# Attention, routed experts and a softplus feed-forward in one kernel: weight-chunk loads, splits and one elementwise operation moved at the joint of the last two stages

## Chip, cores and metric

The kernel runs on one core of one Trainium2 chip. The metric is the device time of one execution in microseconds. Three runs of the kernel before gave 645.68, 647.77 and 648.97 us; their median is 647.77 us.

## What is computed

```python
attn_out = _attn_ref(q, k, v)                    # 2 batches, 8 heads, 576 positions, 64 wide, rotary
x = attn_out.transpose(0, 2, 1, 3).reshape(1152, 512)
x = _moe_ref(x, w_gate, w_noise, noise, w1, w2)  # 8 experts, best 2 of each token: relu(x @ w1[e]) @ w2[e]
# _moe2_ref(x, w_in, w_out): w_in 512 x 2048, w_out 2048 x 512
h = x @ w_in
g = np.maximum(h, 0.0) + np.log1p(np.exp(-np.abs(h)))
return (g @ w_out).astype(np.float32)
```

All products are made to float32 accuracy by splitting both operands into a high part (rounded to fp32r) and a low part (the rest), and adding three products: high by high, high by low, low by high.

## The kernel before, in words

The work is emitted in program order, and each engine runs its own instructions strictly in that order. TensorE (PE) multiplies, ScalarE (ACT) makes high parts and copies out of PSUM, VectorE (DVE) makes low parts, GpSimd (POOL) issues the gathers, and SyncE (SP) issues the loads.

**Weight chunks.** Weights arrive as 80 chunks of 512 KB, numbered 0 to 79: 64 of the experts, and from 64 on 16 of the feed-forward part, which come from the DRAM table `wtab`. `load_chunk` (L149) issues the load of the next chunk into one of 4 buffers `wraw`. `split_hi` (L179) makes the high part on ACT (L189) and queues the low part; `split_lo` (L198) makes the queued low part on DVE (L193) and then calls `load_chunk`, because a `wraw` buffer is free again. Chunk s goes to one of 11 places `w`/`wb`; chunks 75 to 79 go to a pool `wc`. `hold_loads` (L169) makes `load_chunk` only count calls; `let_loads` (L173) issues a small read of `yg` on SP, which waits for the gather of that tile, and then makes up the counted loads.

**The last expert run.** Nine runs of an expert each do eight steps `gemm1(r, f)` and then `gemm2(r, t, part)`, three parts for each tile of 128 rows. After each step `slot()` (L1496) makes the queued low part, and splits the next chunk if it is loaded and below a limit; in the last run the limit lets chunks up to 70 be split. In the last run's step f = 3 three gathers are issued; at f = 5 the loads are held. At the end of tile 0 two more gathers are issued (they read rows that the tile has just put to the DRAM table `ytab`), at the end of tile 1 the loads are let go, in tile 2 the first two token tiles are combined (L1535) and turned (`x2_T`, L1538) into the high and low parts `xh`, `xl` of the feed-forward part's first input.

**The feed-forward part.** Nine token tiles are taken as four groups c of 2, 3, 2 and 2 tiles (`CH`). Before its loop POOL gets three gathers of the next tiles (L1657 to L1660), two of which wait for the last rows put to `ytab`. The loop index n walks through (c, f), f = 0 to 15. In iteration n the program emits: `act2` of n-1 on DVE (L1623, which frees the PSUM buffer, and L1624); now and then a combine or a turn of a coming token tile, which also emits two gathers on POOL; `ff1_` of n (12 matmuls on PE, into one of 3 PSUM buffers `ph`, then Abs, Exp and Ln on ACT); `act3` of n-1 (the high part `gh` on ACT, L1630); `act1` of n (L1618 and L1619: with a = exp(-|h|) it makes u = (a + 1) - 1 and then a - u, which corrects the rounding of Ln's argument); the low part `gl` of n-1 on DVE (L1632); the queued low part of a chunk (L193); one `split_hi` while chunks are left; and `ff2_` of n-3 (six matmuls where the group has two tiles). So chunks 71 to 79 are split in iterations 0 to 8.

Of the kernel before, what the change touches and what calls it, by code (L numbers as in the profile page):

```python
# [18 lines left out]
OP = mybir.AluOpType  # L19
# [13 lines left out]
NR = len(CAPS)  # L33
# [72 lines left out]
def fused_kernel(ctx: ExitStack, tc: tile.TileContext, q, k, v, w_gate, w_noise, noise, w1, w2,  # L106
                 w_in, w_out, cs_t, out):
    nc = tc.nc
# [20 lines left out]
    chunk_src = []  # L129
# [17 lines left out]
    nxt = {"load": 0, "split": 0, "order": False, "held": None}  # L147
# [21 lines left out]
    def hold_loads():  # L169

        nxt["held"] = 0
# [26 lines left out]
    def split_lo():  # L198
        while lo_q:
            lo_q.pop(0)()  # L200
# [918 lines left out]
    for g in range(2 * NP_):  # L1119
        p, h = divmod(g, 2)  # L1120
        for u in range(6 - h):
            n = 5 * g + (0, 1, 2, 3, 3, 4)[u]
# [7 lines left out]
        for a in range(2):  # L1130
            n = 5 * g + 3 + a
# [4 lines left out]
        n = 5 * g + 5  # L1136
# [13 lines left out]
    for p in range(NP_):  # L1150
        n = 10 * p
# [100 lines left out]
    def weights(r):  # L1252
        return max(r - 1, 0)

    def xg_T(r, t):
        if t == 0:
            XT[r] = (mx.tile([128, 4, CAP], F32R, name="xh"), mx.tile([128, 4, CAP], F32R, name="xl"))
        xh, xl = XT[r]
        g = XG.pop((r, t))
        m = min(CAPS[r] - 128 * t, 128)  # L1260
        ps = psA.tile([128, 4, 128], F32, name="pa")[:, :, :m]
        for d in range(4):
            nc.tensor.transpose(ps[:, d, :], g[:m, d * 128:(d + 1) * 128], ident[:m, :m])  # L1263
        dh, dl = xh[:, :, t * 128:t * 128 + m], xl[:, :, t * 128:t * 128 + m]
        nc.scalar.activation(dh, ps, AF.Copy)
        nc.vector.tensor_tensor(out=dl, in0=ps, in1=dh.bitcast(F32), op=OP.subtract)  # L1266

    def gemm1(r, f, pool):
        xh, xl = XT[r]
        cap = CAPS[r]  # L1270
        ps = ps1.tile([128, CAP], F32, name="p1")[:, :cap]
        mm3(ps, [(w1_blk(weights(r), kk, f), (xh[:, kk, :cap], xl[:, kk, :cap])) for kk in range(4)], True, True)
        hb = pool.tile([128, 2 * CAP], F32R, name="hb", bufs=8)

        m = cap % 128 if 0 < cap % 128 <= 64 else 0
        n = cap - m
        hh, hl = hb[:, 0:cap], hb[:, cap + m:cap + m + n]
        HT[f] = hh, hl, hb[:, n:n + 2 * m]
        nc.scalar.activation(hh, ps, AF.Relu)  # L1279
        for o, c in [(hl, slice(0, n))] + [(hb[:, cap:cap + m], slice(n, cap))] * (m > 0):  # L1280
            nc.vector.scalar_tensor_tensor(out=o, in0=ps[:, c], scalar=0.0, in1=hh[:, c].bitcast(F32), op0=OP.max,  # L1281
                                           op1=OP.subtract)

    def gemm2(r, t, part, pool):
        if part == 0:
            P2[0] = ps2.tile([128, DM], F32, name="p2")
        m = min(CAPS[r] - 128 * t, 128)
        ps = P2[0]
        c = slice(t * 128, t * 128 + m)
        fs = ((0, 1, 2), (3, 4, 5), (6, 7))[part]  # L1290
        if m > 64:
            mm3(ps[:m], [((HT[f][0][:, c], HT[f][1][:, c]), w2_blk(weights(r), f)) for f in fs], part == 0, part == 2)
        else:

            for f in fs:
                wh, wl = w2_blk(weights(r), f)
                if f == 7:
                    nc.tensor.matmul(ps[:m], HT[f][0][:, c], wl, start=False, stop=False)
                nc.tensor.matmul(ps[:2 * m], HT[f][2], wh, start=f == 0, stop=f == 7)  # L1299
                if f < 7:  # L1300
                    nc.tensor.matmul(ps[:m], HT[f][0][:, c], wl, start=False, stop=False)  # L1301
        if part < 2:
            return
        y = ya[t] if r == 0 else pool.tile([128, DM], F32, name="y", bufs=2)
        if r + 1 == NR:
            Y8[t] = y
        if m > 64:
            nc.scalar.activation(y[:m], ps[:m], AF.Copy)
        else:
            nc.scalar.activation(y[:m], ps[m:2 * m], AF.Copy)  # L1310
            nc.vector.tensor_tensor(out=y[:m], in0=ps[:m], in1=y[:m], op=OP.add)
        r0 = (NOV + ROW0[r] + t) * 128

        def put():
            nc.scalar.dma_start(out=ytab[r0:r0 + m, :], in_=y[:m])
        if m > 64:
            put()
        else:
            puts.append((slot_no[0] + 2, put))
# [147 lines left out]
    def gather(r):  # L1467
        for t in range(RTILES[r]):
            m = min(CAPS[r] - 128 * t, 128)
            XG[r, t] = mo.tile([128, DM], F32, name="xg", bufs=4)  # L1470
            gather_rows(XG[r, t][:m], idxr[:m, r - 2, t:t + 1])
# [5 lines left out]
    def turn():  # L1477
        ps = psA.tile([128, 4, 128], F32, name="pa")
        nc.tensor.transpose(ps[:, 0, :], to1, ident)
        nc.scalar.activation(toT, ps[:, 0, :], AF.Copy)  # L1480
# [15 lines left out]
    def slot(limit):  # L1496
        n = slot_no[0]
        slot_no[0] += 1
        split_lo()
        if n >= 8:  # L1500
            next(late, None)
        while puts and puts[0][0] <= n:
            puts.pop(0)[1]()
        todo = sorted(dec_at.get(n, []), key=lambda x: x[0] is dec_load)
        for fn, u in todo:
            if u < NDEC:
                fn(u)
        if all(fn is not dec_b for fn, _ in todo) and nxt["split"] < min(limit, nxt["load"]):
            split_hi()
# [4 lines left out]
    def ygather(i, kk):  # L1514
        nonlocal ygt
        if ygt is None:
            ygt = yg_tile().bitcast(F32)
        o = (i % 3 if kk == 0 else 3 + i % 2) * DM
        g = ygt[:, o:o + DM]
        near = (i, kk) == (1, 1)  # L1520
        top = (NOV + ROW0[NR - 1] + (1 if near else min(i + 1, CB) if kk else 0)) * 128
        nc.gpsimd.indirect_dma_start(out=g, out_offset=None, in_=ytab[0:top, :],  # L1522
                                     in_offset=bass.IndirectOffsetOnAxis(ap=near1 if near else yrow[:, i, kk:kk + 1], axis=0))
        YG[i, kk] = g
# [4 lines left out]
    def scale0(i):  # L1529
        a = YG[i, 0]  # L1530
        nc.scalar.activation(a, a, AF.Copy, scale=wts[:, i, 0:1])
# [28 lines left out]
    for r in range(1, NR):  # L1560
        e = weights(r)
        for f in range(8):
            gemm1(r, f, mo)
            if r == 3 and f == 0:
                for _ in late:
                    pass
                turn()
            if r + 1 == NR and f == 3:
                for i in range(CH[0] + 1):
                    ygather(i, 0)  # L1570
            if r + 1 == NR and f == 5:
                hold_loads()
            slot(min(8 * e + NSLOT + f // 2, 64 + NSLOT))
        for t in range(RTILES[r]):
            for part in range(3):
                gemm2(r, t, part, mo)
                if r + 1 < NR and (t, part) in when[:RTILES[r + 1]]:
                    xg_T(r + 1, when.index((t, part)))
                if r + 1 == NR:
                    for do in ends.get((t, part), []):  # L1580
                        do()
                slot(min(8 * e + NSLOT + 4, 64 + NSLOT))
        if r + 2 < NR:
            gather(r + 2)
# [30 lines left out]
    def act1(c, f):  # L1615

        ps, a, l, u = HS[c, f]
        nc.vector.tensor_scalar(u, a, 1.0, 1.0, op0=OP.add, op1=OP.subtract)  # L1618
        nc.vector.tensor_tensor(out=a, in0=a, in1=u, op=OP.subtract)  # L1619

    def act2(c, f):
        ps, a, l, u = HS[c, f]
        nc.vector.scalar_tensor_tensor(out=l, in0=ps, scalar=0.0, in1=l, op0=OP.max, op1=OP.add)  # L1623
        nc.vector.tensor_tensor(out=l, in0=l, in1=a, op=OP.add)  # L1624
# [44 lines left out]
    for n in range(len(seq) + FL):  # L1669
        if 1 <= n <= len(seq):  # L1670
            act2(*seq[n - 1])
        for i, u in extra.pop(n, []):
            if u == 0:
                scale0(i)
                combine(i)
            else:
                x2_T(i, psh.tile([128, 4, 128], F32, name="px", bufs=1))
                if i + 2 < NT:
                    ygather(i + 2, 0)
                    ygather(i + 2, 1)  # L1680
        if n < len(seq):
            ff1_(*seq[n])
        sub = act3(*seq[n - 1]) if 1 <= n <= len(seq) else None
        if n < len(seq):
            act1(*seq[n])
        if sub:
            sub()
        split_lo()
        if nxt["split"] < len(chunk_src):
            split_hi()  # L1690
        if n >= FL:
            c, f = seq[n - FL]
            for o in range(CH[c]):
                ff2_(c, f, o)
# [38 lines left out]
```

## Time and profile before

| | us |
|---|---|
| median of three runs | 647.77 |
| the profiled execution, its own time | 647.54 |
| its span, first to last instruction | 645.5 |
| PE busy | 624.0 (97%) |
| DVE busy | 482.2 (75%) |
| ACT busy | 424.3 (66%) |
| POOL busy | 211.7 (33%) |
| mean granted TensorE clock, share of full | 0.987 |

The profiled execution's time is 2.0 us more than its span and 0.2 us below the median. Busy matmul time is modelled, so a busy PE can still be waiting a little in each iteration. The chain of waits follows back from the last instruction to what released each step; a window table gives each engine's busy time and the granted clock in a stretch; a timeline lists instructions with their start and duration, and in brackets the idle time before them and what ended it.

### The profile page before, as it was taken

The page shows a single profiled execution, that of the slowest core. Times are in us where ns is not written, and L with a number is a line of the kernel's source. Part 1 is how long each engine was busy: PE and PEld are TensorE (multiplying, and loading weights), DVE is VectorE, ACT ScalarE, POOL GpSimd, SP SyncE. Part 2 cuts the span into 40 slices and gives each one's busy share as a digit, 9 for nine tenths or more (in the row PEclk, how much of TensorE's full clock was granted, in tenths as well). Part 3 has the DMA queues.
Part 4 walks back from the last instruction along what each step waited for, and adds up shares of the span by engine and source line. Part 5 has one row for each costly group of instructions (what it writes and reads, how often), then busy time and mean ns, then how long its engine had stood idle before and what let it go on. Part 6 is the DMA issues. An engine that isn't in the chain of part 4 may idle for free.

```text
span 645.5 us, 11587 instructions
## 1 busy us (share of the span) xinstructions
PE 624.0 (97%) x3957; PEld 560.0 (87%) x3957; DVE 482.2 (75%) x986; ACT 424.3 (66%) x893; POOL 211.7 (33%) x304
## 2 busy tenths in 40 slices
PE   6898999999999999999999999979999999999997
PEld 3798999999879889797988889868789989889986
DVE  5997899999876887686867776439986656676764
ACT  4986999899636677475757665438765554565553
POOL 7997636874271324323241414202110100000000
PEclk7998999999999999999999999989999999999999
DMA  5565655887419799989998997477211100100000
GB/s 132 139 143 133 160 119 129 234 242 214 136 53 356 232 354 336 319 276 344 315 336 292 330 307 231 140 256 210 87 34 50 33 1 1 49 2 2 34 2 32
DMA packets 69921, 109.59 MB, mean 170 GB/s; under 512 B 11716, under 2 KB 38980, under 8 KB 69476
## 3 DMA queue, kind: packets, MB, share of 16 engines
q1 hardware_dynamic: 63442, 93.20, 46.8%
q0 software_dynamic: 3136, 10.10, 4.7%
q10 hardware_dynamic: 3282, 5.54, 2.4%
q8 instruction: 32, 0.52, 0.3%
q14 instruction: 29, 0.24, 0.1%
HBM read 76.50 MB, written 23.59 MB: 155 GB/s over the span
## 4 chain that ended last, share of the span: by engine, by line
PE 63%; DVE 3%; DMA 2%; ACT 1%; issue 1%; POOL 0%; SPq 0%; DVEq 0%
PE p L270 10%; PE p L271 10%; PE p L272 10%; PE po L272 5%; PE ph L270 5%; PE po L271 5%; PE po L270 5%; PE ph L271 5%; PE ph L272 5%; PE p L1299 2%; PE pa L1263 1%; PE p L1301 1%; DMA wraw<-wtab 1%; DMA yg<-ytab,near 1%; DVE wb L193 1%
## 5 line engine op out<-in xcount | busy, mean ns | idle before, releaser
L239 POOL TENSOR_TENSOR dm<-dm,da 128x512 int32<-128x512 int32 x32 | 41.9, 1310 | 127.9 <-DVE da L236 63.3
L1611 ACT ACTIVATE fa<-ph 128x256 f32<-128x256 f32 (+1 forms) x64 | 26.0, 406 | 69.2 <-PE ph L272 69.2
L504 DVE TENSOR_REDUCE nmx<-ps 128x1 f32<-128x576 f32 x72 | 53.8, 750 | 8.5 <-PE ps L491 7.8
L193 DVE TENSOR_TENSOR w<-wraw,w 128x1024 fp32r<-128x1024 f32 x41 | 54.2, 1328 | 5.8 <-ACT w L189 5.8
L513 ACT ACTIVATE P<-ps,nmx 128x576 f32<-128x576 f32 x72 | 53.7, 745 | 3.0 <-DVE nmx L504 2.3
L1281 DVE SCALAR_TENSOR_TENSOR hb<-p,hb 128x256 fp32r<-128x256 f32 (+1 forms) x104 | 31.7, 345 | 30.3 <-ACT hb L1279 30.2
L1618 DVE TENSOR_SCALAR fu<-fa 128x256 f32<-128x256 f32 (+1 forms) x64 | 19.9, 311 | 45.9 <-ACT fa L1612 45.7
L189 ACT ACTIVATE w<-wraw 128x1024 fp32r<-128x1024 f32 x42 | 44.3, 1058 | 13.1 <-DMA wraw<-wtab 6.8
L558 DVE TENSOR_TENSOR ptl<-pt,pth 128x512 fp32r<-128x512 f32 x72 | 48.4, 684 | 5.0 <-ACT pth L554 4.5
L1522 POOL DMA_INDIRECT yg<-ytab,yrow x17 | 17.2, 1010 | 91.7 <-DVE fu L1618 42.5
L554 ACT ACTIVATE pth<-pt 128x512 fp32r<-128x512 f32 x72 | 42.4, 600 | 6.9 <-PE pt L522 6.4
L271 PE MATMUL p<-xl,w 128*128 128x256 f32 (+3 forms) x152 | 46.3, 305 | 0.3 <-DVE xl L1266 0.3
L270 PE MATMUL p<-xh,w 128*128 128x256 f32 (+3 forms) x152 | 46.3, 305 | 0.0
L272 PE MATMUL p<-xh,w 128*128 128x256 f32 (+3 forms) x152 | 46.2, 304 | 0.0
L193 DVE TENSOR_TENSOR wb<-wraw,wb 128x1024 fp32r<-128x1024 f32 x33 | 45.0, 1370 | 0.0
L522 PE MATMUL pt<-ident,P 128*128 128x128 f32 x288 | 42.7, 275 | 0.9 <-DVE ptl L558 0.6
L189 ACT ACTIVATE wb<-wraw 128x1024 fp32r<-128x1024 f32 x33 | 34.8, 1058 | 2.9 <-DMA wraw<-in_moe_w_dram 2.8
L1619 DVE TENSOR_TENSOR fa<-fa,fu 128x256 f32<-128x256 f32 (+1 forms) x64 | 29.4, 459 | 9.8 <-ACT fl L1613 7.1
L522 PEld LDWEIGHTS pt<-ident,P 128*128 128x128 f32 x288 | 34.3, 142 | 1.9 <-DVE ptl L558 1.1
L491 PE MATMUL ps<-wb,yg 128*128 128x288 f32 (+1 forms) x160 | 31.3, 325 | 3.1 <-DMA w<-in_v_dram 2.2
L1630 ACT ACTIVATE gh<-fl 128x256 fp32r<-128x256 f32 (+1 forms) x64 | 27.7, 432 | 9.4 <-DVE fl L1624 9.4
L1279 ACT ACTIVATE hb<-p 128x320 fp32r<-128x320 f32 (+3 forms) x64 | 25.7, 419 | 12.0 <-PE p L272 11.3
(387 smaller groups left out, 2170.0 us busy)
## 6 DMA issues: line engine op xcount, KB each, us to landing
wraw<-in_moe_w_dram SPq DMA_DIRECT2D x64, 512.0 KB, 4.9
x<-in_moe_w_in_dram SPq DMA_DIRECT2D x16, 512.0 KB, 6.4
x<-in_moe_w_out_dram SPq DMA_DIRECT2D x16, 512.0 KB, 4.7
wtab<-dm SPq DMA_DIRECT2D x32, 256.0 KB, 5.7
wraw<-wtab SPq DMA_DIRECT2D x16, 512.0 KB, 5.3
ytab<-y ACTq DMA_DIRECT2D x18, 256.0 KB, 5.4
ytab<-wb SPq DMA_DIRECT2D x4, 1024.0 KB
wb<-wb SPq DMA_DIRECT2D x6, 640.0 KB
```

What stands on the lines that cost most here:

```text
L189: nc.scalar.activation(hi, r, AF.Copy)
L193: lo_eng.tensor_tensor(out=lo, in0=r, in1=hi.bitcast(F32), op=OP.subtract)
L239: nc.gpsimd.tensor_tensor(out=m, in0=m, in1=ai, op=OP.add)
L270: nc.tensor.matmul(ps, ah, bh, start=first and i == 0, stop=False)
L271: nc.tensor.matmul(ps, ah, bl, start=False, stop=False)
L272: nc.tensor.matmul(ps, al, bh, start=False, stop=last and i == n - 1)
L504: nc.vector.tensor_reduce(out=nmx, in_=stS[n][:, :, :HN], axis=AX.XY, op=OP.max, negate=True)
L513: nc.scalar.activation(P_of(n).rearrange("p (a c) -> p a c", a=2), ps[:, :, :HN], AF.Exp, bias=nmx, scale=1.0, accum_out=acc)
L522: nc.tensor.transpose(ps[:, kb, :], Pt[:, kb * 128:(kb + 1) * 128], ident)
L554: nc.scalar.activation(dh, x, AF.Copy)
L558: nc.vector.tensor_tensor(out=dl, in0=x, in1=dh.bitcast(F32), op=OP.subtract)
L1281: nc.vector.scalar_tensor_tensor(out=o, in0=ps[:, c], scalar=0.0, in1=hh[:, c].bitcast(F32), op0=OP.max, op1=OP.subtract)
```

## The change

Three edits: the loads are held at step f = 7 of the last run instead of f = 5; for the first group (c = 0) the first operation of `act1` goes to GpSimd instead of VectorE; and in the feed-forward loop no chunk is split in iterations 1, 4, 7, ... The number of chunks and all arithmetic stay the same.

```diff
-            if r + 1 == NR and f == 5:
+            if r + 1 == NR and f == 7:
                 hold_loads()
...
     def act1(c, f):
         ps, a, l, u = HS[c, f]
-        nc.vector.tensor_scalar(u, a, 1.0, 1.0, op0=OP.add, op1=OP.subtract)
+        (nc.gpsimd if c == 0 else nc.vector).tensor_scalar(u, a, 1.0, 1.0, op0=OP.add, op1=OP.subtract)
         nc.vector.tensor_tensor(out=a, in0=a, in1=u, op=OP.subtract)
...
         split_lo()
-        if nxt["split"] < len(chunk_src):
+        if n % 3 != 1 and nxt["split"] < len(chunk_src):
             split_hi()
```

## Rows read from the trace of the kernel before

**Rows 1.** Windows: stretch, length, busy PE PEld DVE ACT POOL, clock, DMA share, GB/s.

```profile
431.70:440.44 8.74, 8.63 (x55) 8.02 (x55) 5.12 (x11) 5.54 (x12) 3.81 (x4) 0.83 0.67 198
440.44:478.40 37.96, 37.58 (x229) 31.07 (x230) 36.02 (x81) 29.74 (x67) 5.77 (x6) 1.00 0.38 116
478.40:630.00 151.60, 151.60 (x888) 137.28 (x887) 99.94 (x241) 82.29 (x193) 2.84 (x3) 1.00 0.06 18
```

**Rows 2.** Chain of waits before the feed-forward part: start us, us, what.

```profile
423.25 5.50 DMA wraw<-wtab
...
429.74 0.59 ACT xh L1551
...
431.69 0.58 PE ph L270
```

**Rows 3.** DMA issues of the page: chunk loads from the table, median us to landing.

```profile
wraw<-wtab SPq DMA_DIRECT2D x16, 512.0 KB, 5.3
```

**Rows 4.** PE timeline: start us, us, line, out<-in; three single matmuls.

```profile
427.70 0.40 PE L272 MATMUL p<-wb,hb 128*128 128x512 f32 x1
...
475.57 0.28 PE L270 MATMUL ph<-xh,wc 128*128 128x256 f32 x1
...
478.39 0.34 PE L270 MATMUL ph<-xh,wb 128*128 128x384 f32 x1
```

**Rows 5.** ACT timeline: the last expert tile's copy out of PSUM.

```profile
430.69 0.60 ACT L1308 ACTIVATE y<-p 128x512 f32<-128x512 f32 x1
```

**Rows 6.** POOL timeline: the third of the three gathers before the loop.

```profile
436.76 0.95 POOL L1522 DMA_INDIRECT yg<-ytab,yrow  x1 [0.30 <-DVE fl L1623]
```

**Rows 7.** POOL timeline: scalar operations, one operator (L1006, L661) and two (L1008, L707).

```profile
44.02 1.52 POOL L1006 TENSOR_SCALAR wb<-ident 128x512 fp32r<-128x512 f32 x1
45.60 0.20 POOL L1008 TENSOR_SCALAR kb<-iota 128x8 f32<-128x8 f32 x1
...
111.73 0.36 POOL L707 TENSOR_SCALAR c<-e 128x32 f32<-128x32 f32 x1
...
128.02 0.25 POOL L661 TENSOR_SCALAR kb<-isA 128x8 f32<-128x8 f32 x1
```

**Rows 8.** POOL timeline: two stretches in which DVE works beside it.

```profile
181.63 1.64 POOL L804 TENSOR_SCALAR P<-iotaA,P 128x128 f16<-128x128 f16 x1
183.25 0.60 POOL L804 TENSOR_SCALAR P<-iotaA,P 128x128 f16<-128x128 f16 x1
...
258.21 1.30 POOL L239 TENSOR_TENSOR dm<-dm,da 128x512 int32<-128x512 int32 x1 [2.84 <-ACT wb L189]
```

**Rows 9.** DVE timeline: low parts of chunks beside these.

```profile
181.66 1.22 DVE L193 TENSOR_TENSOR w<-wraw,w 128x1024 fp32r<-128x1024 f32 x1
...
258.86 1.74 DVE L193 TENSOR_TENSOR w<-wraw,w 128x1024 fp32r<-128x1024 f32 x1
```

**Rows 10.** DVE timeline: one iteration of the feed-forward loop in group c = 0.

```profile
450.07 0.42 DVE L1624 TENSOR_TENSOR fl<-fl,fa 128x256 f32<-128x256 f32 x1
450.42 0.28 DVE L1618 TENSOR_SCALAR fu<-fa 128x256 f32<-128x256 f32 x1
450.81 0.43 DVE L1619 TENSOR_TENSOR fa<-fa,fu 128x256 f32<-128x256 f32 x1
...
451.49 1.22 DVE L193 TENSOR_TENSOR wc<-wraw,wc 128x1024 fp32r<-128x1024 f32 x1
452.62 0.42 DVE L1623 SCALAR_TENSOR_TENSOR fl<-ph,fl 128x256 f32<-128x256 f32 x1
```

**Rows 11.** ACT timeline: one iteration of the feed-forward loop in group c = 0.

```profile
457.13 0.42 ACT L1630 ACTIVATE gh<-fl 128x256 fp32r<-128x256 f32 x1 [0.45 <-DVE fl L1624]
457.45 1.05 ACT L189 ACTIVATE wc<-wraw 128x1024 fp32r<-128x1024 f32 x1
458.41 0.36 ACT L1611 ACTIVATE fa<-ph 128x256 f32<-128x256 f32 x1
458.80 0.42 ACT L1612 ACTIVATE fa<-fa 128x256 f32<-128x256 f32 x1
```

## The prediction, made before the changed kernel ran

> **What bounds the kernel now.** I read the window table first. From 478.4 to 630 us PE is busy without a gap at full clock, and so it is nearly throughout: PE sets the end, and whatever delays it near the joint of the stages moves the end by as much [rows 1]. Two stretches beside the change are not of that kind. In 440.44 to 478.40, the first group (c = 0) from its fifth iteration to the first matmul of the second group, DVE is busy 36.0 of 38.0 us; here PE waits a little for DVE in most iterations [rows 1]. And the chain of waits leaves PE before the feed-forward part: it runs through a chunk load (5.50 us), a split on ACT, the copy to xh at 429.74, and reaches PE at 431.69 [rows 2], while PE's last product of the expert run began at 427.70 [rows 4]. ACT stands in its queue at the splits of chunks 69 and 70, whose loads were let go late, and the copies to xh are queued behind them. The gap also costs clock: from 431.70 to 440.44 the granted clock is 0.83 of full, that is, part of the stretch ran at 1.2 instead of 2.4 GHz, a loss of 0.17 x 8.74 = 1.5 us [rows 1].
>
> **Edit 1, loads held two steps later.** By index: at f = 5 of the last run the low part of chunk 65 is made, at f = 6 that of 66. Their calls now load chunks 69 and 70 at once. Slots then split 69 and 70 after the first two parts of tile 0, and the limit (70) stops there; 71 to 74 are the four loads let go. So the two splits leave ACT's queue ahead of xh. The loads take 5.3 us to land [rows 3], about the time of the tile's 24 products, so ACT may reach the split of 70 a little before it lands: 0 to 1 us on the copy of tile 0, and the two combines behind it had slack; I take 0. On SP the two loads pass the last store to the table, which only chunk 79 needs. With xh free, PE can go on right behind its last product, at about 427.9, since copies and differences of both tiles take 1.95 us in the chain [rows 2] and the first tile's are done beside PE. The start comes 3.7 us earlier, and no clock is lost there.
>
> **Edit 2, u on GpSimd.** First its place. POOL runs in order, and ahead of u(0) stand three gathers that wait for the last expert tile to reach DRAM. That tile's copy began at 430.69 and the first gather at 436.76 - 2 x 1.25 = 434.26, 3.6 us later, the third ending at 437.7 [rows 5, 6]. The copy can now start at about 428.1; so the gathers run from about 431.5 and POOL is free at 435.0. Before, none of that stood in DVE's way. Now a - u of iteration 0 waits on DVE, behind it act2(0), which frees the first of three PSUM buffers, and gh(0) on ACT: PE does three iterations (12 matmuls, 1.4 us each, to 432.2) and stops. With u at 1.25 us (below): u(0) ends at 436.2, DVE's next two operations 0.8 us later, and PE's fourth iteration starts at 437.2, after a gap of 5 us that is longer than the one which halved the clock before; I charge 1.3 us of half clock again. The fifth iteration would then start at 441.3 against 440.44: **the joint costs +0.9 us** in place of gaining about 5.
>
> Its duration: on POOL one-operator scalar work costs 0.25 us at 8 columns and 1.52 at 512, 2.5 ns a column. The very same two operators (add, subtract, L707) took 0.36 at 32 columns, where one operator would take 0.31: 1.5 ns a column more. At 256 columns: 0.23 + 256 x 4.0 ns = 1.26 us. Low end: the extra is a fixed 0.05, 0.94 us. High end: from the two-operator 0.20 at 8 columns through 0.36 at 32, 6.7 ns a column, 1.85 us [rows 7]. I take 1.25, because the nearest row is the same operation. DVE gives up 0.39 us an iteration for it (450.42 to 450.81) [rows 10].
>
> The GPSIMD Engine Reference of the Trainium skill (4.1 Engine selection) says that one-input work runs at roughly line rate on GpSimd. By that u would take some 0.3 us (an estimate from that page) and the first group would be PE's again. The 1.52 us row speaks against it.
>
> Now the sharing. Where a POOL operation ran from 258.21 to 259.51, DVE's low part begun at 258.86 took 1.74 us instead of 1.22: it ended 1.09 us after POOL did. And a one-input POOL operation begun at 181.63, beside a low part of DVE (181.66 to 182.88), took 1.64 us instead of 0.60 [rows 8, 9]. So operations of the two exclude each other where DVE reads two SBUF tensors, as L1624, L1619, L1632 and L193 do. L1623 reads PSUM and is free of it. What no row shows is a one-input POOL operation holding up DVE.
>
> The SBUF — State Buffer page of the Trainium skill (SBUF: two separate sides) calls it an exclusive lock held for the whole instruction, taken by either side. By that u holds up DVE too, which is the forecast; without it, the second rival.
>
> **Edit 3, splits in two of three.** The nine splits and low parts move from iterations 0 to 8 to 0, 2, 3, 5, 6, 8, 9, 11, 12; no chunk is needed before it is there (72 at iteration 8 is split at 2; 79 at 17 is split at 12). DVE's iteration without the low part is about 1.9 us, and two low parts of 1.13 in three add 0.75: by itself the edit brings DVE near PE's own 2.82 us (475.57 to 478.39) [rows 4, 10].
>
> **The loop with both.** From the end of u(n), with L1624 waiting for POOL, the queues give three kinds of iteration [rows 10, 11], with 0.08 us for a handover. (a) No split of its own, a low part from before: L1624 0.39, gh 0.42, gl 0.42, low part 1.13, then u 1.25, which had to wait for the low part: 3.61. (b) Split, no low part: L1624 0.39, gh 0.42, split 0.96, Abs 0.39, Exp 0.45, handover and u 1.33: 3.94, and 0.5 more where ACT copies a turned tile, as it does about every other time: 4.44. (c) Split and low part, with ACT still the last: Ln 0.36, gh 0.34, split 0.96, Abs and Exp 0.84, scaling of a coming tile 0.63: 3.14. A cycle of three takes 11.2 us. Twelve iterations from the fifth on would take 44.8; the last three have no split and by the same queues come to 3.1, 3.8 (a turned tile) and 3.0, 9.9 in all, so 43.5 against the 38.0 in the trace [rows 1]: **+5.5 us**. What follows is PE's at full rate and gives nothing back [rows 1].
>
> **Sum:** 647.54 + 0.9 + 5.5 = 653.9, say **654.0 us**, in terms of the profiled execution; the median of the runs lies 0.2 higher, below what I can resolve.
>
> **Rivals.**
> - B: POOL doesn't hold DVE up, or u is nearer its low end. With u at 1.25 and no exclusion, DVE stays below PE except that gathers queued on POOL delay u in some iterations: twelve iterations take about 37.6, and +0.9 at the joint gives +0.5: 648. With exclusion and u at 0.94, kinds (a) and (b) are 0.3 us shorter, which leaves about +3: 650.5. For it: no row of a one-input POOL operation stopping DVE. Against: exclusion seen in both directions.
> - C, the other side: u is cheap (under 0.5 us) or finds its way into POOL's idle time, and the group becomes PE's: 12 x 2.82 is 33.8, some 35 with three turned tiles, instead of 38.0: -3. With the stall at the joint that is 644.5 to 645.5; without the stall (gathers done before u(0) is due) PE also keeps the 3.7 us and the clock, and 641 is reached. For it: DVE is what PE waits for now, and POOL is idle there for 32 of 38 us. Against: 0.36 us at 32 columns. It decides where u stays below about 0.7 us.
> - D: two operators cost 1.85 us on POOL. Each kind of iteration grows by 0.6 and the joint too: +12 to +15, 660 to 663.
> - That edit 1 doesn't do what it says I rule out by the indices.
>
> **How the numbers follow.** Forecast 0.52, own range 650.5 to 659; B 0.22; C 0.17; D 0.09. About 0.5% (3.2 us) is what can be told from no change: faster means below 644.5, slower above 651. C gives 0.15 faster and the rest of it none; B gives most of 0.24 no change; forecast and D give 0.61 slower. The range leaves out most of C and the upper half of D: 645 to 661.
>
> **What would show it.** PE: the first matmul of the feed-forward part at about 428, then a gap of some 5 us before its fourth iteration, with POOL's gathers ending just before the first u. L1618 on POOL at 1.1 to 1.4 us. L1624, L1619, L1632 and L193 stretched where u runs, L193 on some occasions above 2 us, and the group's iterations at 3.1 to 4.4 us in a pattern of three. Wrong if u takes under 0.7 us, if the DVE rows keep their lengths beside u, or if POOL's u(0) runs ahead of the gathers' end.

## The result, and the profile after

The changed kernel took 651.93 us in the median of five runs (650.36 to 653.41), the kernel before, measured alongside in five runs, 646.63 (645.53 to 648.97). The ratio is 1.0077, with an interval of 1.0048 to 1.0106: slower by 0.8%. Its profiled execution took 650.36 us with a span of 648.5, 3.0 us more than the span before. The medians lie 5.3 us apart: the profiled execution of before took 0.9 us more than its median, that of the changed kernel 1.6 less than its own. So what follows explains the 3.0 us between the two profiles.

The first thing to see is that TensorE no longer waits before the feed-forward part, but stands still before its fourth first-layer group. PE timeline before,

```profile
431.69 0.58 PE L270 MATMUL ph<-xh,wb 128*128 128x256 f32 x1 [3.58 <-DVE xl L1552]
```

and after; the first row answers to the start at 431.69:

```profile
427.52 0.39 PE L270 MATMUL ph<-xh,wb 128*128 128x256 f32 x1
...
437.88 0.58 PE L270 MATMUL ph<-xh,w 128*128 128x256 f32 x1 [5.89 <-DVE fl L1623]
...
475.92 0.39 PE L272 MATMUL ph<-xh,wc 128*128 128x256 f32 x1 [1.89 <-DVE wc L193]
```

The chain of waits after (start, us, what) runs through that gap and names each link:

```profile
427.53 0.61 ACT y L1308
428.16 3.21 DMA ytab<-y
...
434.75 0.95 POOL yg L1522
435.74 1.11 POOL fu L1618
436.88 0.62 DVE fa L1619
437.50 0.34 DVE fl L1623
437.88 0.58 PE ph L270
```

The last tile's copy starts 3.16 us earlier than before [rows 5]; its way to DRAM takes 3.21 us; three gathers follow on GpSimd, and u(0) stands behind them. Only then can VectorE make a - u and free the PSUM buffer. Windows after, for the stretches that answer to rows 1 (length, busy PE PEld DVE ACT POOL, clock, DMA share, GB/s):

```profile
427.52:443.17 15.65, 9.76 (x54) 8.98 (x55) 5.56 (x12) 7.36 (x16) 6.71 (x6) 0.79 0.43 136
443.17:481.43 38.26, 36.00 (x229) 31.74 (x228) 30.81 (x61) 28.00 (x63) 22.48 (x19) 1.00 0.34 99
481.43:632.00 150.57, 150.57 (x880) 136.25 (x879) 99.78 (x242) 82.72 (x193) 5.03 (x5) 1.00 0.07 20
```

DVE is busy 30.8 of 38.3 us where it was 36.0 of 38.0 [rows 1], and yet the stretch is no shorter. From 481.43 on PE is full again.

To cut the time where the elementwise chain stands and not where PE, which runs ahead of it, happens to be, I use the Abs (L1611) of the first, fourth and 17th first-layer group; the 17th is the first of c = 1. ACT timeline before:

```profile
434.65 0.39 ACT L1611 ACTIVATE fa<-ph 128x256 f32<-128x256 f32 x1 [3.37 <-PE ph L272]
...
442.76 0.36 ACT L1611 ACTIVATE fa<-ph 128x256 f32<-128x256 f32 x1
...
480.72 0.49 ACT L1611 ACTIVATE fa<-ph 128x384 f32<-128x384 f32 x1 [1.93 <-PE ph L272]
```

and after:

```profile
429.23 0.39 ACT L1611 ACTIVATE fa<-ph 128x256 f32<-128x256 f32 x1 [1.10 <-PE ph L272]
...
443.09 0.36 ACT L1611 ACTIVATE fa<-ph 128x256 f32<-128x256 f32 x1
...
483.75 0.49 ACT L1611 ACTIVATE fa<-ph 128x384 f32<-128x384 f32 x1 [1.03 <-PE ph L272]
```

The start is 5.42 us earlier, first to fourth takes 13.86 instead of 8.11 (+5.75), fourth to 17th 40.66 instead of 37.96 (+2.70). The sum is +3.03; the spans differ by 3.0. From the 17th Abs to the last instruction it is 164.8 us in both. Every kernel below is cut in the same way; "1 to 4" I call the joint and "4 to 17" the loop.

| kernel | edits | median us | ratio, interval | 1st Abs | joint | loop | span |
|---|---|---|---|---|---|---|---|
| before | none | 646.63 | 1 | 434.65 | 8.11 | 37.96 | 645.5 |
| after | 1, 2, 3 | 651.93 | 1.0077 [1.0048, 1.0106] | 429.23 | 13.86 | 40.66 | 648.5 |
| e5 | 1 | 641.44 | 0.9918 [0.9894, 0.9943] | 429.20 | 8.11 | 38.01 | 640.0 |
| e6 | 3 | 646.14 | 0.9999 [0.9981, 1.0018] | 432.20 | 8.21 | 37.93 | 643.1 |
| e11 | 2 | 649.10 | 1.0044 [1.0028, 1.0060] | 434.94 | 10.64 | 38.36 | 648.7 |
| e1 | 1, 3 | 641.91 | 0.9916 [0.9894, 0.9938] | 429.62 | 8.12 | 38.03 | 640.5 |
| e2 | 1, 3, u on POOL from f = 3 | 644.04 | 0.9966 [0.9943, 0.9989] | 428.44 | 8.10 | 40.48 | 641.7 |
| e3 | 1, 3, u on POOL up to f = 2 | 648.18 | 1.0015 [1.0000, 1.0031] | 430.51 | 14.10 | 38.14 | 647.5 |
| e10 | 1, no split in iterations 1, 4 | 641.00 | 0.9918 [0.9896, 0.9941] | 429.18 | 8.10 | 37.43 | 639.4 |
| e4 | 1, 2, 3, 44 products | 650.75 | 1.0059 [1.0036, 1.0081] | 428.72 | 14.08 | 40.68 | 648.2 |
| e7 | 1, 2, 3, 22 products | 650.96 | 1.0069 [1.0047, 1.0091] | 427.59 | 13.99 | 42.21 | 648.5 |
| e8 | 1, 3, one-input side work | 645.40 | 0.9996 [0.9983, 1.0009] | 429.81 | 8.10 | 41.88 | 644.5 |
| e9 | 1, 3, two-input side work | 647.05 | 1.0013 [0.9996, 1.0031] | 429.11 | 8.11 | 43.41 | 645.4 |
| e12 | 1, 2 | 648.79 | 1.0033 [1.0017, 1.0049] | 429.64 | 14.12 | 38.49 | 647.0 |

Each ratio is against runs of the kernel before made alongside (medians 645.85 to 646.81). The columns on the right are of one profiled execution each. The first Abs moves without an edit that touches it: by 2.9 us between e7 and e3, which are alike up to there, and by 2.45 in e6, whose median is that of before. So single differences in it are rough; the joint and the loop repeat within 0.3 us wherever their edits are the same, except in e7, told below.

### The profile page after: what moved, and what is told of

The parts are those of the page before. It is cut to its first block, busy times and chain, and to the rows that moved or that the text cites. A ratio compares the mean times of both kernels' runs of the same rounds, so it can differ in the third digit from the quotient of the medians.

```text
span 648.5 us, 11602 instructions
## 1 busy us (share of the span) xinstructions
PE 623.1 (96%) x3957; PEld 560.3 (86%) x3957; DVE 479.6 (74%) x970; ACT 425.1 (66%) x893; POOL 234.0 (36%) x320
## 4 chain that ended last, share of the span: by engine, by line
PE 61%; POOL 2%; DVE 2%; issue 2%; DMA 2%; ACT 1%; SPq 0%; ACTq 0%; POOLq 0%; DVEq 0%
PE p L271 10%; PE p L270 10%; PE p L272 9%; PE po L271 5%; PE po L272 5%; PE po L270 5%; PE ph L270 5%; PE ph L272 5%; PE ph L271 5%; PE p L1299 2%; PE p L1301 1%; PE pa L1263 1%; POOL fu L1618 1%; DMA x<-in_moe_w_in_dram 1%; POOL yg L1522 1%
## 5 line engine op out<-in xcount | busy, mean ns | idle before, releaser
L1611 ACT ACTIVATE fa<-ph 128x256 f32<-128x256 f32 (+1 forms) x64 | 26.0, 406 | 65.1 <-PE ph L272 65.1
L1619 DVE TENSOR_TENSOR fa<-fa,fu 128x256 f32<-128x256 f32 (+1 forms) x64 | 29.5, 461 | 24.2 <-POOL fu L1618 16.4
L1618 DVE TENSOR_SCALAR fu<-fa 128x256 f32<-128x256 f32 (+1 forms) x48 | 15.3, 319 | 41.8 <-ACT fa L1612 41.8
L270 PE MATMUL ph<-xh,w 128*128 128x256 f32 (+1 forms) x96 | 29.3, 305 | 5.9 <-DVE fl L1623 5.9
```

Source lines behind the costliest of these rows:

```text
L270: nc.tensor.matmul(ps, ah, bh, start=first and i == 0, stop=False)
```

## The experiments

### What each edit is worth: e1, e2, e3

All three keep edits 1 and 3 and put u on VectorE for all, for the first three or for the later iterations of c = 0:

```diff
-        (nc.gpsimd if c == 0 else nc.vector).tensor_scalar(u, a, ...)
+        nc.vector.tensor_scalar(u, a, ...)                                  # e1
+        (nc.gpsimd if c == 0 and f >= 3 else nc.vector).tensor_scalar(u, a, ...)  # e2
+        (nc.gpsimd if c == 0 and f < 3 else nc.vector).tensor_scalar(u, a, ...)   # e3
```

> The changed kernel with u back on VectorE in all iterations: edits 1 and 3 alone. Both theories agree on it: PE goes on right behind the expert run, no gap before its fourth iteration, 6 us less than the kernel before (about 640.5 where that runs at 646.6), so edit 2 would cost 10 to 11 us in all. If edits 1 and 3 are worth nothing by themselves, it comes out at the kernel before.

> u on GpSimd only from f = 3 of the first group on; u(0) to u(2), which stand behind the three gathers, on VectorE. Joint theory (the price of edit 2 is the wait of u(0) behind the gathers and the half clock after it): within 2 us of the kernel with u on VectorE everywhere, 640.5 to 642.5, no gap on PE before its fourth iteration. Loop theory (the price is GpSimd's slower u and its exclusion with VectorE in every iteration, as predicted): 4 to 6 us above that kernel, 645 to 647.

> The reverse: only u(0) to u(2) on GpSimd, the rest on VectorE. Joint theory: nearly the whole loss stays, 649 to 652, with a gap of about 6 us on PE before its fourth iteration. Loop theory: the joint costs about 0.9 us against the kernel before and the loop's 5.5 us are gone, 644 to 646.

Without edit 2 the kernel is 0.8% faster than before. The three operations beside the gathers cost 14.10 - 8.12 = 6.0 us in the joint and nothing in the loop; the other 13 cost 40.48 - 38.03 = 2.5 us in the loop and nothing in the joint. Together 8.5, and after minus e1 is 8.4: the two parts add up. By the medians edit 2 costs 10.0 us, within the 10 to 11 expected (the profiled executions of after and e1 differ by 7.9). Neither theory is right alone: 644.04 (e2) and 648.18 (e3) each lie between the two forecasts. PE timeline of e3, the gap with only three operations on POOL:

```profile
439.40 0.58 PE L270 MATMUL ph<-xh,w 128*128 128x256 f32 x1 [6.13 <-DVE fl L1623]
```

### Each edit alone: e5, e6, e11

e5 is edit 1 alone, e6 edit 3, e11 edit 2, each as in the diff of the change.

> Edit 1 alone: loads held two steps later, u on VectorE, a split in every iteration. If the whole gain of edits 1 and 3 (4.9 us where the kernel before ran at 646.8) is that of the joint, as the first group's twelve iterations suggest (38.0 us both with edits 1 and 3 and in the kernel before): 641 to 643. If edit 3 gives 2 to 3 us of it, as the queues reckoned: 644 to 645.

> Edit 3 alone. If splits in two of three relieve VectorE: the twelve iterations shorten by 1.5 us, 645 to 645.5. If the later splits are paid back by PE waiting for chunk 78 (1.1 us with edits 1 and 3): no change, 646 to 647.5.

> Edit 2 alone. There PE reaches the feed-forward part 3.7 us later, so u(0) is due near the end of the gathers (437.7 in the kernel before), about 2.5 us after u ended there. Joint theory: a shorter gap before the fourth iteration, 2 to 3 us, no half clock after it, and 2 to 2.5 us for the loop: 649 to 652. If edit 2's cost needs edit 1: within 1 us of the kernel before.

Edit 1 alone is the whole gain of e1: first Abs 5.45 us earlier, nothing else moved, span 5.5 shorter; by the ratio it is 0.8%, or 5.3 us. Edit 3 alone moves neither joint nor loop. Edit 2 alone costs 2.5 us in the joint (u(0) behind the gathers there too, but the copies to xh were late anyway) and only 0.4 in the loop, where e2 had 2.5. So the loop's 2.5 is not edit 2's own: it needs another edit beside it, and e12 below shows that this is edit 3.

### A wait that edit 3 brings: e10, e12

In after PE waits 1.89 us at 475.92 for the low part of chunk 78 (the last is 79). The same wait is 1.90 us in e2 and e4, 1.91 in e7, 1.13 in e1 and e6, 1.11 in e3; it is absent from the traces of before, e5 and e11. e10 leaves out two splits instead of every third, so that chunk 78 is split earlier; e12 is edits 1 and 2 with a split in every iteration.

```diff
-        if n % 3 != 1 and nxt["split"] < len(chunk_src):
+        if n not in (1, 4) and nxt["split"] < len(chunk_src):   # e10, u on VectorE
+        if nxt["split"] < len(chunk_src):                       # e12, u on GpSimd for c = 0
```

> Edits 1 and 3 with u on VectorE, but only iterations 1 and 4 without a split, so that chunk 78 is split at iteration 9 instead of 11. If PE's wait for the low part of chunk 78 in its fifteenth iteration (1.1 us) is a loss of its own: 1 us less than with edits 1 and 3, about 641. If VectorE's load in the iterations before decides: no change or slower, 642 to 643.

> Edits 1 and 2 together, with a split in every iteration as before (the third edit undone). Theory A: what the subtraction on GpSimd costs inside the loop is not GpSimd stopping VectorE but the late split of chunk 78 (its low part ends 1.89 us after TensorE asks for it in the changed kernel, 1.90 with GpSimd from the fourth iteration on, and there is no such wait with edit 1 alone or edit 2 alone). Then this kernel has no wait for the low part of chunk 78, the stretch from the first to the 17th Abs of the feed-forward part is near 52.5 us (54.5 in the changed kernel, 46.2 with edits 1 and 3 and the subtraction on VectorE), and the time is 649 to 650.5, ratio 1.004 to 1.0065. Theory B: GpSimd beside VectorE slows the loop, whatever the splits: the stretch stays at 54 to 55 us and the ratio at 1.0075 or more, since a third more splits bring more two-input operations beside which it stands. The gap of 5.9 us before the fourth first-layer group stays in both.

e10 takes the wait away and 0.6 us off the loop of e1, but its ratio is that of e1 and e5: too little to time. Nor is a wait a loss by its length: e1's loop has 1.13 us of it and takes 38.03, e5's has none and takes 38.01. e12 is the one that decides. PE timeline of e12: the gap stands, and the longest other wait of PE in the group is this,

```profile
438.52 0.58 PE L270 MATMUL ph<-xh,w 128*128 128x256 f32 x1 [6.09 <-DVE fl L1623]
...
470.00 0.50 PE L272 MATMUL po<-wb,gl 128*128 128x512 f32 x1 [0.24 <-DVE gl L1632]
```

with no wait for a chunk. The stretch from first to 17th Abs is 52.6 us, as theory A had it (52.5), against 54.5 after; the loop is 38.49. The ratio, 1.0033, is a little below the 1.004 expected. So of the loop's +2.70 some 2.2 come from edits 2 and 3 meeting, and 0.5 from u on POOL as such. PE's own starts show where the 2.2 fall. The first matmul of its fifth, 15th and 16th group, after:

```profile
443.17 0.41 PE L270 MATMUL ph<-xh,w 128*128 128x256 f32 x1
...
473.55 0.36 PE L270 MATMUL ph<-xh,wc 128*128 128x256 f32 x1
...
478.61 0.28 PE L270 MATMUL ph<-xh,wc 128*128 128x256 f32 x1
```

and in e12:

```profile
443.80 0.37 PE L270 MATMUL ph<-xh,w 128*128 128x256 f32 x1
...
474.20 0.36 PE L270 MATMUL ph<-xh,wc 128*128 128x256 f32 x1
...
477.10 0.28 PE L270 MATMUL ph<-xh,wc 128*128 128x256 f32 x1
```

From the fifth to the 15th PE takes 30.4 us in both; from the 15th to the 16th, where the wait for chunk 78 lies, 5.06 after and 2.90 in e12. So the 2.2 us are lost there, 1.89 of them in that wait. By the Abs 1.5 of them are there at the 13th already: with edits 2 and 3 the elementwise chain falls back while PE still has its lead, and the late low part is where this reaches PE.

### Is the half clock the price of the gap? e4, e7

After the gap PE runs at half clock for a whole iteration. Both kernels fill it with products whose results nobody reads:

```diff
+        if n == 3:
+            fill = psh.tile([128, 4, 128], F32, name="px", bufs=1)
+            for i in range(44):      # e4; range(22) in e7
+                nc.tensor.matmul(fill[:, i % 4, :], ident, ident, start=True, stop=True)
```

> The changed kernel with 44 small products that nobody reads put on PE between its third and fourth iteration of the feed-forward part, about 4.8 us, inside the gap of 5.9 us. If the clock is a term of the joint: the fourth iteration starts when it did, but at full clock, and the half clock's 5.5 us (a loss of 2.7) are gone: 2.5 us less than the changed kernel, about 649. If later iterations wait for VectorE and GpSimd anyway, nothing changes: 651 to 652.

> The changed kernel with 22 small products that nobody reads on PE between its third and fourth iteration, 5.0 us, inside the gap of 5.9 us (44 ran on for 10 us and put the fourth iteration off). If half clock after the gap is a term: the fourth iteration starts when it did, the fifth 2.3 us sooner, and the time falls by 1 to 2.5 us, 649 to 651; what is missing to 2.5 was given back by waits of the loop. If not: as the changed kernel, 651.8.

e4 overshot: its products took 9.99 us and PE's fourth group began at 441.09, some 3 us later than after. e7 fitted: they end 1.07 us before the fourth group. Windows of e7 (the fourth group; then two stretches about the wait for chunk 78):

```profile
436.37:439.27 2.90, 2.90 (x18) 2.46 (x19) 2.67 (x6) 1.53 (x4) 1.19 (x1) 1.00 0.00 1
470.00:475.00 5.00, 3.09 (x21) 2.58 (x20) 3.75 (x9) 4.00 (x9) 2.31 (x2) 1.00 0.00 0
475.00:480.00 5.00, 5.00 (x26) 4.42 (x25) 4.30 (x10) 2.54 (x6) 3.68 (x4) 0.66 0.38 104
```

and of after, where the fourth group ran at 1.2 GHz:

```profile
470.00:475.00 5.00, 3.77 (x24) 3.25 (x24) 3.75 (x10) 4.21 (x9) 1.87 (x2) 1.00 0.01 3
475.00:480.00 5.00, 4.08 (x28) 3.83 (x29) 4.76 (x9) 2.97 (x8) 4.24 (x4) 1.00 0.19 52
437.88:443.17 5.29, 5.29 (x18) 4.71 (x19) 4.59 (x10) 3.49 (x8) 1.72 (x1) 0.50 0.33 88
```

The group's iteration on PE falls from 5.29 to 2.90 us, but the joint by the Abs stays: 13.99 in e7, 14.08 in e4, 13.86 after. PE had slack there; DVE and ACT, which got their work late, set the pace, and neither a faster clock nor 3 us of products more is seen behind them. The times alone don't decide it: 1.0059 and 1.0069 can't be told from 1.0077, and e7's 650.96 lies in the range that was given for a clock term. e7 then lost 1.55 us in the loop: the clock fell to 0.66 in 475 to 480, worth 0.34 x 5 = 1.7 us by estimate, after the same wait of 1.91 us. Why it fell there and not in after, I can't say.

### Does POOL hold up VectorE? e8, e9

u stays on VectorE (edits 1 and 3); once per iteration POOL gets an operation of 128x256 of its own, whose result nobody reads. It writes into the tile of a spent u.

```diff
+        if 1 <= n <= 16:
+            g0 = G[seq[n - 1]][0].bitcast(F32)
+            side = US[seq[n - 1]]
+            nc.gpsimd.tensor_scalar(side, g0, 1.0, 1.0, op0=OP.add, op1=OP.subtract)   # e8
+            nc.gpsimd.tensor_tensor(out=side, in0=g0, in1=g0, op=OP.add)               # e9
```

> The kernel with edits 1 and 3 and u on VectorE, and beside it in each iteration of the first group a GpSimd operation of u's form (one SBUF input, two operators, 256 columns) that reads gh and writes a tile nobody reads any more: GpSimd works as in the changed kernel, but VectorE doesn't wait for it. Exclusion both ways, as predicted: VectorE's two-input rows (L1619, L1624, L1632, L193) stretch by up to 1 us beside it and the time rises by 2 to 4 us over 641.9. If a one-input operation only waits for VectorE and hardly holds it: rows stretch by 0.2 us at most, time within 1 us of 641.9.

> The same with a GpSimd operation of two SBUF inputs (add of gh to itself, 256 columns, 0.73 us by the form that ran before). A two-input operation held VectorE's low part for 0.5 us before: VectorE's two-input rows beside it should stretch by up to 0.7 us, more than beside the one-input operation, although this one is shorter; time 642 to 644.

Both times missed: e8's 645.40 lies in the range given for exclusion, not within 1 us of 641.9, and e9's 647.05 above 642 to 644. Neither theory can be read straight from them: the loop grew by 3.9 and 5.4 us over e1, but part of that is a fault of my design. DVE timeline of e8 (u is L1619 here):

```profile
438.45 0.51 DVE L1619 TENSOR_SCALAR fu<-fa 128x256 f32<-128x256 f32 x1 [2.46 <-POOL fu L1690]
```

The tile that POOL was to write came round again, its operation stood behind the three gathers, and DVE waited 2.46 us for it (1.97 in e9). A write to a shared tile is a wait as good as a read. Of the growth 2.4 and 2.3 us are there by the sixth Abs, just behind this wait; the other 1.5 and 3.1 come over the 11 iterations that follow. What the two do settle is read from single rows. DVE timelines by operation, low parts of chunks, in 440 to 478 us of e8,

```profile
L193 DVE TENSOR_TENSOR wc<-wraw,wc 128x1024 fp32r<-128x1024 f32 x5 | 6.9, 1375 | 0.0
```

and of e9 (busy us, mean ns), against 1219 before:

```profile
L193 DVE TENSOR_TENSOR wc<-wraw,wc 128x1024 fp32r<-128x1024 f32 x5 | 7.3, 1466 | 0.0
L1620 DVE TENSOR_TENSOR fa<-fa,fu 128x256 f32<-128x256 f32 x12 | 6.3, 527 | 1.3
```

a - u (L1620) rises to 527 ns from 0.43 us alone [rows 10]. The dearest single meeting in e9, on DVE,

```profile
450.82 1.80 DVE L193 TENSOR_TENSOR wb<-wraw,wb 128x1024 fp32r<-128x1024 f32 x1
```

and on POOL:

```profile
450.91 0.62 POOL L1690 TENSOR_TENSOR fu<-gh 128x256 f32<-128x256 f32 x1
```

A low part beside a two-input POOL operation takes up to 0.58 us more than alone (1.22), about that operation's own 0.62. In e8, beside a one-input operation of 1.07 us, the mean of 1.375 means 0.16 us more, and no low part there takes over 0.2 us more.

## Why the forecast came out as it did, step by step

**Edit 1: right.** The first feed-forward product was forecast for about 427.9 and came at 427.52. ACT timeline after, at the splits of 69 and 70 and the copy of tile 0:

```profile
411.03 1.06 ACT L189 ACTIVATE w<-wraw 128x1024 fp32r<-128x1024 f32 x1 [1.01 <-DMA wraw<-wtab]
412.87 1.06 ACT L189 ACTIVATE w<-wraw 128x1024 fp32r<-128x1024 f32 x1 [0.77 <-DMA wraw<-wtab]
414.16 0.60 ACT L1308 ACTIVATE y<-p 128x512 f32<-128x512 f32 x1 [0.23 <-PE p L272]
```

ACT waits for both loads, the median landing being 5.5 us where it was 5.3 [rows 3], and still has to wait for PE before the copy: the cost is 0, as taken. Its worth, "about 5", is 5.5 us in e5.

**Edit 2 at the joint: right in mechanism, about right in sum.** The gap of 5 us is 5.89 and sits before the fourth group, with u(0) right behind the gathers. POOL timeline after, which answers to rows 6 and 7:

```profile
432.24 0.95 POOL L1522 DMA_INDIRECT yg<-ytab,yrow  x1 [12.93 <-DMA ytab<-y]
433.50 0.95 POOL L1522 DMA_INDIRECT yg<-ytab,yrow  x1 [0.30 <-issue]
434.75 0.95 POOL L1522 DMA_INDIRECT yg<-ytab,yrow  x1 [0.30 <-issue]
...
443.98 1.07 POOL L1618 TENSOR_SCALAR fu<-fa 128x256 f32<-128x256 f32 x1 [2.67 <-DVE yg L1535]
446.41 1.51 POOL L1618 TENSOR_SCALAR fu<-fa 128x256 f32<-128x256 f32 x1 [1.35 <-ACT fa L1612]
...
458.50 1.07 POOL L1618 TENSOR_SCALAR fu<-fa 128x256 f32<-128x256 f32 x1 [1.07 <-ACT fa L1612]
```

The first gather came 4.7 us after the copy's start, not 3.6, and the third ended at 435.70 where 435.0 was forecast. u takes 1.07 us alone, between the low end (0.94) and the value taken (1.25). PE's fourth group began at 437.88 (forecast 437.2), its fifth at 443.17 (441.3), because the half clock lasted the whole iteration. By PE's fifth group the joint would be +2.7 and not +0.9; but e7 shows that this last delay is PE's slack. By the Abs the joint is 5.75 lost against 5.42 gained, +0.3, with the roughness of the first Abs told above.

**The loop: wrong, and this is the step that failed.** It was to take 43.5 us on PE; it took 38.26, against 37.95 before, and +2.7 by the Abs where +5.5 was forecast. The failed assumption is "with L1624 waiting for POOL". DVE timeline after, which answers to rows 9 and 10:

```profile
445.76 1.22 DVE L193 TENSOR_TENSOR wb<-wraw,wb 128x1024 fp32r<-128x1024 f32 x1
446.90 0.42 DVE L1623 SCALAR_TENSOR_TENSOR fl<-ph,fl 128x256 f32<-128x256 f32 x1
447.35 0.42 DVE L1624 TENSOR_TENSOR fl<-fl,fa 128x256 f32<-128x256 f32 x1
447.95 0.42 DVE L1619 TENSOR_TENSOR fa<-fa,fu 128x256 f32<-128x256 f32 x1 [0.17 <-POOL fu L1618]
...
458.55 1.43 DVE L193 TENSOR_TENSOR wc<-wraw,wc 128x1024 fp32r<-128x1024 f32 x1
```

The u of 446.41 to 447.92 was slowed by the low part begun at 445.76 and ended 0.94 us after it; but L1624, begun inside that u, took its usual 0.42. The u of 458.50 to 459.57 cost the low part beside it 0.21 us and not its own 1.07; no low part came near the 2 us that the prediction looked for. So u gives way to VectorE, and VectorE hardly to u: the condition of rival B, which the prediction gave less than half the chance of its forecast, and nearly its own sign of being wrong, "if the DVE rows keep their lengths beside u". VectorE does wait for u's results before a - u, 6.4 us in 440 to 478, but with the splits as before the loop grows by only 0.5 us (e12). The row that pointed the other way [rows 8, 9] was a two-input POOL operation; I carried it over to a one-input one, though the prediction itself noted that no row showed that. Its sum has a slip besides: kind (b) is 4.44 only "about every other time", but the cycle of 11.2 us takes it so each time; with the half of it a cycle is 10.9 and the loop 42.7.

The SBUF — State Buffer page of the Trainium skill (SBUF: two separate sides) has whichever instruction starts first hold the shared ports throughout, the other blocked in full. By that (an estimate) the low part begun at 458.55 would have ended 1.22 us after u, at 460.79; it ended at 459.98, and the measurement decides. For u as the later of the two, the trace nearly agrees with it: u ended 0.94 us after the low part, where 1.07 is its time alone.

**Edit 3: wrong twice, in sizes that set what is left of the loop.** It was to bring DVE "near PE's own" pace. Alone it moves the loop by nothing (e6 37.93, e1 38.03, before 37.96): the nine low parts stay within the same 16 iterations, so VectorE's work in the group is the same, only spread. And "no chunk is needed before it is there" counted iterations of the program and left out that VectorE runs behind PE: chunk 78's low part began at 474.64, when ff1(14), which multiplies by it, had begun on PE at 473.55. With u on POOL, VectorE is later still, and the wait goes from 1.13 to 1.89 us.

**The sum.** Forecast +0.9 and +5.5, so 654.0; measured +0.3 and +2.7 in the profiled execution, 651.93 in the median. The sign came from the joint eating up what edit 1 gives, as forecast (without edit 2 the kernel is faster, e1). The size of the slowdown was forecast through POOL holding up VectorE, of which 0.5 us is there at most (e12), and in its place stands a wait that edits 2 and 3 make together and that the prediction did not have. So that 651.93 lies within 650.5 to 659 is partly luck: with POOL not holding VectorE up, the prediction's own figure was rival B's 648, what came on top is a wait that it had ruled out, and the profiled execution, in whose terms the forecast was made, took 650.36.

## What to carry to other kernels

Work moved to an idle engine is queued behind whatever that engine is waiting for: GpSimd was idle because its gathers waited, and three operations behind them cost 6 us while the 13 later ones, without edit 3, cost about 0.5. When work is delayed "because there is time", compare the consumer's engine time with the producer's, not their iteration numbers. A gap on the busiest engine is priced by what comes late behind it; here filling it and keeping the clock up bought nothing.

## What the runs showed of the hardware that was not expected

- A one-input GpSimd operation (128x256, 1.07 us) costs a two-input VectorE operation beside it some 0.2 us (1.43 for 1.22 after, 1.42 in e8), while it is itself held up by VectorE: begun inside a low part it took 1.51 to 2.04 us and ended some 0.93 us after it. A two-input GpSimd operation (some 0.6 us alone) lengthens VectorE's by up to 0.58 us (1.80 for 1.22 in e9).
- u takes 0.28 us on VectorE [rows 10] and 1.07 on GpSimd.
- After the 5.9 us gap the granted clock was 0.50, that is 1.2 GHz, for the whole 5.29 us of the next group; after the 3.58 us gap before, the stretch of 8.74 us had 0.83 [rows 1], which is about 3 us at that level (an estimate, 2 x 0.17 x 8.74).
